# Long-convolution block with feed-forward on one core: new layout of the short convolution, row pairs in the second product, two more tiles transposed by DMA, and a new order

## The chip, the cores and the metric

One core of a Trainium2 chip. The metric is the device time of one execution in microseconds (us). TensorE is called PE (PEld is its loading of weights), VectorE DVE, ScalarE ACT, GpSimd POOL, and SyncE SP; SP here only issues DMAs. PSUM has eight banks of 512 32-bit words per partition.

## The reference

Inputs and output are bfloat16; S = 2048 tokens, D = 640 channels, F = 1728.

```python
def _A_ref(q, k, v, shift_k, ssm_k, ssm_D):
    k_shift = sum of k delayed by t (t = 0..3) * shift_k[:, t]      # causal, 4 taps
    kv = k_shift * v
    y = irfft(rfft(kv, 2S) * rfft(ssm_k, 2S))[:S]                   # long causal convolution per channel
    y = y + kv * ssm_D
    return q * y

def _B_ref(x, w1, b1, w2):
    h = x @ w1 + b1
    return (h * tanh(softplus(h))) @ w2

x = A_q
h = x + _A_ref(layernorm(x), A_k, A_v, A_shift_k, A_ssm_k, A_ssm_D)
out = h + _B_ref(layernorm(h), B_w1, B_b1, B_w2)
```

## The kernel before

**Stages.** The channels are five blocks of 128 (written m or b below), in three chunks: blocks 0 and 1, blocks 2 and 3, block 4. The long convolution is a Fourier transform in two stages of matmuls, a product, and an inverse in two stages:

- `k1pe`, `k1ev`: the filter `A_ssm_k` of one block, transposed on PE (eight transposes per half unit), and copied from PSUM. `dadd` then adds the skip term `ssm_D` to tap 0, one row of 128 values.
- `ktpe`, `ktev`, `ktsh`: the same for `A_k`, in groups of 32 channels; POOL makes a copy shifted by one column for the taps that reach into the tile before.
- `wsh`, `coef`, `cfpe`: band matrices of the short filter's taps, built by POOL from a mask and `coef`. `kspe` multiplies them with the transposed k: for each of 20 channel groups and four steps `a` one matmul of 128 columns and one of 96. `kv` (DVE) multiplies the result in PSUM with v.
- `s1kpe`/`s1vpe`: stage 1 of the transform for filter and signal, pairs of matmuls of 64 weight columns each. `s2kpe`/`s2vpe`: stage 2, with the table G (4 MB, loaded as `d_g0` to `d_g7`).
- `sw`: DMAs that copy the filter's spectrum with partitions swapped in pairs. `p2`, `p1`: products of the signal's spectrum with the swapped and the plain filter, by DVE or POOL.
- `i1pe`: first inverse stage. `i2pa`, `i2pb`, `i2pc` (one per chunk, for each of 16 token tiles): second inverse stage, with the table t2m (1 MB).
- Per token tile of 128 tokens: `ln1` (first norm's statistics), `ln1p`, `lnx`, `y` (PSUM copy), `wb` (times the normed x), `h` (plus x), `bn`, `pow`, `hc` (second norm), and a transpose into `lnhT`.
- Feed-forward in units of 256, 256, 512, 512, 512 tokens: `m1pe` (13 column blocks of w1, five matmuls each), `hb` (ACT: Mish), `m1pex` (the last 64 of the 1728 columns, two groups side by side in PE's columns), `m2pe` (per tile two halves of 320 columns, 14 matmuls each), `res` (plus h), `d_out` (store).

A name ends in x or y for the two halves of a unit. Evacuations of PSUM (names with `ev`, and `y`) are copies by ACT or DVE.

**Transposes of the second norm.** Tiles 0 to 3 (units 0 and 1) are transposed on PE (`trpe`, five transposes at line 850) and copied by ACT or DVE (`trev`). Tiles 4 to 15 go by a transposing DMA on SP's queue (`trd`, line 839).

**The 64-row remainder of the second product.** w2 has 13 blocks of 128 rows and one of 64. The last matmul of each `m2pe` (line 916) uses all 128 rows of `hbx`, whose halves hold different tokens, against w2 padded with zeros in the other half:

```python
_, lhs, h = last64[t2]
nc.tensor.matmul(po[:, 0:d1 - d0], lhs, w2h[:, d0:d1] if h else w2[:, 13, d0:d1], start=False, stop=True)
```

The zeros are written by POOL (`w2z`, `w2hz`).

**Order.** The text `ORDER` names some 1030 steps, each with its engine (t PE, a ACT, v DVE, p POOL, d SP's DMA queue, s ACT's DMA queue). Each engine works through its own steps in that order; a planner (`_schedule`) with estimated durations merges them into one sequence of emission and gives out the PSUM banks. DMAs of SP are issued in the order's sequence, and each waits for its inputs at SP. DVE and POOL products are kept from running at the same time by a small POOL copy (`turn`).

Of the kernel before, what the change touches and what calls it, by code (L numbers as in the profile page):

```python
# [16 lines left out]
S = 2048  # L17
D = 640
# [8 lines left out]
d_id:s d_sk:s wz:v d_dr:s cz:v d_go:d d_n2:d wm:t fz0:t d_n0:d k1pe2x:t warm:a k1ev2x:a d_n3:d k1pe2y:t d_n1:d cfpe:t d_n4:d k1pe0y:t k1ev0y:a  # L27
k1pe0x:t k1ev2y:v dadd2:v s1kpe2_0x:t k1ev0x:v kz:p coef:v s1kpe2_2x:t s1kpe2_1x:t s1kpe2_1y:t s1kev2_1x:v s1kev2_0x:v s1kev2_1y:v s1kpe2_3y:t
s1kev2_3y:a k1pe3x:t k1ev3x:a s1kev2_2x:a k1pe1x:t k1ev1x:v k1pe1y:t w2hz:p dadd0:p wsh0:p dadd1:p k1pe3y:t dadd3:p k1pe4y:t k1ev1y:v k1pe4x:t
k1ev3y:v k1ev4x:v dadd4:p s1kpe1_2y:t k1ev4y:a s1kpe1_3x:t s1kpe1_0x:t s1kev1_0x:v s1kpe1_0y:t s1kpe1_1x:t s1kev1_1x:v s1kpe0_1x:t s1kpe1_3y:t  # L30
s1kpe4_0y:t s1kev1_2y:a s1kpe2_2y:t s1kev1_3x:a d_k3:d d_k2:d d_x0:d s1kev0_1x:a s1kev1_0y:v s1kev1_3y:a s1kev2_2y:a s1kpe3_0x:t s1kpe0_2y:t
s1kev0_2y:a s1kpe0_1y:t s1kev3_0x:a s1kpe2_3x:t s1kev2_3x:a ktpe3y:t s1kpe0_2x:t s1kpe4_2x:t s1kev4_2x:a s1kev4_0y:v ln1_2:v s1kev0_1y:v ln1_1:v
s1kpe4_1x:t s1kpe0_0x:t s1kev4_1x:a s1kpe4_2y:t s1kpe1_2x:t s1kev0_0x:v s1kpe0_0y:t d_k1:d d_g4:d s1kev1_2x:a d_k0:d d_g5:d s1kpe3_2x:t ktpe0y:t
s1kev0_2x:a ktpe1y:t d_v1:d ktev0y:v ktpe4y:t ktev3y:v s1kpe4_0x:t ktev1y:v ktev4y:v s1kev4_2y:a s1kev0_0y:a s1kev3_2x:a s1kpe3_1y:t s1kev4_0x:a
s1kev3_1y:a s1kpe3_3x:t s1kpe3_0y:t s1kpe4_1y:t s1kev3_3x:a s1kpe0_3y:t s1kpe4_3y:t s1kpe2_0y:t s1kpe4_3x:t s1kev0_3y:v s1kev2_0y:v s1kev4_1y:a
ln1_3:v s1kev3_0y:a s1kev4_3x:a wsh1:p s1kpe3_2y:t ln1p1:p s1kpe3_1x:t s1kpe1_1y:t ktsh1:p wsh3:p s1kpe0_3x:t s1kpe3_3y:t s1kev3_1x:a ktpe2y:t
s1kev0_3x:a s1kev4_3y:a s1kev3_2y:v s1kev1_1y:v ktpe4x:t ktpe3x:t ktev3x:v ktpe1x:t s1kev3_3y:a ktev1x:v ln1_0:v ktpe0x:t s2kpe_14y:t d_g6:d d_g0:d
ktev2y:a ktpe2x:t d_g7:d d_g1:d ktev4x:a s2kpe_13x:t s2kev_13x:a s2kpe_15y:t s2kpe_12y:t s2kev_12y:a ktev0x:a s2kev_15y:a kspe4_1x:t ktev2x:v kv4_1x:v
# [104 lines left out]
class _Op:  # L143
    def __init__(self, name, opts, deps, allocs, uses, emit, prio, lat):
# [12 lines left out]
        self.start = None  # L157
        self.eng = None
        self.done = False
        self.tiled = name.startswith("s1") and "pe" in name or name.startswith("m1pex")  # L160
# [14 lines left out]
def _schedule(ops):  # L175
# [7 lines left out]
    for word in ORDER:  # L183
# [6 lines left out]
        for rt in o.allocs:  # L190
            t, rt.slot = rt.ring.free()
            est = max(est, t)
# [34 lines left out]
def _dve1(n):  # L227
    return 0.06 + 0.001045 * n
# [740 lines left out]
```

## Time and profile before

| what | value |
|---|---|
| runs | 224.22, 224.60, 224.79 us; median 224.6 |
| profiled execution | 224.86 us, span 223.1 us |
| granted clock of PE | 1.00 |
| busy: PE, DVE, ACT, POOL | 214.7, 146.2, 134.4, 65.7 us |
| HBM read, written | 20.45 MB, 2.62 MB |
| first transposes of the filter on PE | at 5.71 us |
| first evacuation of a stage-1 product | at 9.50 us |
| last matmul of the first inverse stage | 89.5 us |
| PE's last matmul | 219.8 to 220.0 us |

Busy time is the sum over an engine's instructions; on PE the ends of matmuls are modelled, so a matmul that waits may count as busy. Where many matmuls follow each other, the distance from start to start is the better measure. Where instructions of ACT or DVE follow each other without a gap, the length of the whole run over their number is the step.

### The profile page before, as it was taken

To read this page: it belongs to the slowest core of one execution; us is meant where nothing else is said; L and a number is where in the kernel's file an instruction comes from. 1 tells how busy PE (TensorE), PEld (TensorE's weight loads), DVE (VectorE), ACT (ScalarE), POOL (GpSimd) and SP (SyncE) were. 2 spreads that over 40 slices of the span, in tenths; PEclk is the share of its full clock that TensorE was granted. 3 is DMA by queue.
4 is the path that set the end of the run, shared out by engine and by line. 5 is a ranking of instruction groups with operands and counts; after the bars stand their busy time and mean duration, and the time that the engine had idled before them with its cause. 6 is when DMAs were issued, how large, how long until landed. Compare 5 with 4: busy or idle time off the path is not lost.

```text
span 223.1 us, 6218 instructions
## 1 busy us (share of the span) xinstructions
PE 214.7 (96%) x2598; PEld 162.1 (73%) x2598; DVE 146.2 (66%) x317; ACT 134.4 (60%) x268; POOL 65.7 (29%) x106
## 2 busy tenths in 40 slices
PE   7998899999999999999999999999999999999994
PEld 2988899999877999988887644576645445675773
DVE  0699989999999998999788898974400000004023
ACT  2689989999999999888870446800053454330000
POOL 1271950005596007235767714320000000000000
PEclk9999999999999999999999999999999999999999
DMA  6999991075999999100001401043350000000024
GB/s 214 388 408 424 408 413 69 3 203 193 277 290 283 319 351 347 62 3 0 3 0 32 88 0 31 0 91 60 88 179 0 1 0 3 0 0 0 32 82 153
DMA packets 27342, 30.68 MB, mean 138 GB/s; under 512 B 9393, under 2 KB 23730, under 8 KB 26930
## 3 DMA queue, kind: packets, MB, share of 16 engines
q1 hardware_dynamic: 26880, 30.10, 41.1%
q8 instruction: 20, 0.33, 0.6%
q10 hardware_dynamic: 338, 0.18, 0.3%
q14 instruction: 8, 0.07, 0.1%
q0 software_dynamic: 96, 0.00, 0.0%
HBM read 20.45 MB, written 2.62 MB: 103 GB/s over the span
## 4 chain that ended last, share of the span: by engine, by line
PE 64%; DVE 13%; DMA 7%; ACT 7%; POOL 5%; issue 2%; SPq 0%; DVEq 0%; ACTq 0%; POOLq 0%
PE ps L915 21%; PE ps L898 19%; ACT uv L419 6%; DMA x<-in_A_q_dram 5%; PE ps L743 4%; PE ps L744 4%; PE ps L652 3%; PE ps L543 2%; PE ps L571 2%; DMA rn<-in_A_ssm_k_dram 2%; DVE st L776 2%; DVE st L822 2%; PE ps L595 2%; POOL r L782 2%; PE ps L916 2%
## 5 line engine op out<-in xcount | busy, mean ns | idle before, releaser
L915 PE MATMUL ps<-rn,uv 128*128 128x320 bf16 (+2 forms) x416 | 61.1, 299 | 0.2 <-DVE x L921 0.2
L903 ACT ACTIVATE uv<-ps,b1s 128x512 bf16<-128x512 f32 (+1 forms) x65 | 35.4, 610 | 39.1 <-PE ps L898 38.5
L898 PE MATMUL ps<-G 128*128 128x512 bf16 (+1 forms) x325 | 58.6, 337 | 0.0
L915 PEld LDWEIGHTS <-uv 128*128 128x128 bf16 x416 | 40.2, 98 | 17.5 <-issue 0.4
L419 ACT CAST uk<-ps 128x512 bf16<-128x512 f32 (+1 forms) x96 | 48.7, 702 | 2.6 <-PE ps L544 1.6
L898 PEld LDWEIGHTS <-G 128*128 128x128 bf16 x325 | 31.2, 98 | 23.9 <-issue 1.1
L921 DVE TENSOR_TENSOR xb<-ps,xb 128x320 bf16<-128x320 f32 (+2 forms) x12 | 5.7, 487 | 36.3 <-PE ps L916 35.8
L419 ACT CAST uv<-ps 128x512 bf16<-128x512 f32 (+2 forms) x57 | 28.7, 845 | 0.0
L921 DVE TENSOR_TENSOR xa<-ps,xa 128x320 bf16<-128x320 f32 x12 | 5.9, 488 | 21.6 <-PE ps L916 21.6
L827 POOL TENSOR_TENSOR r<-ve,mhalf 128x1 f32<-128x1 f32 x16 | 10.0, 630 | 32.7 <-DVE ve L824 32.7
L743 PE MATMUL ps<-a,uv 128*128 128x128 bf16 x160 | 18.8, 219 | 0.2
L421 DVE CAST uk<-ps 128x512 bf16<-128x512 f32 (+1 forms) x27 | 17.2, 669 | 1.4 <-PE ps L744 0.9
L743 PEld LDWEIGHTS <-uv 128*128 128x128 bf16 x160 | 17.9, 113 | 0.0
L421 DVE CAST uv<-ps 128x512 bf16<-128x512 f32 (+1 forms) x25 | 15.3, 677 | 0.0
L685 PE MATMUL ps<-uv,G 128*128 128x64 bf16 (+1 forms) x256 | 12.8, 197 | 0.8
L685 PEld LDWEIGHTS <-G 128*128 128x128 bf16 x256 | 11.1, 96 | 3.1 <-issue 2.1
L600 DVE TENSOR_TENSOR ra<-ps,rb 128x512 bf16<-128x512 f32 x20 | 12.5, 684 | 0.3 <-PE ps L596 0.3
L419 ACT CAST rb<-ps 128x512 bf16<-128x512 f32 (+1 forms) x28 | 10.6, 495 | 2.7 <-PE ps L803 2.7
L652 PE MATMUL ps<-uk,G 128*128 128x160 bf16 x128 | 12.1, 230 | 0.0
L782 POOL TENSOR_TENSOR r<-ve,mhalf 128x1 f32<-128x1 f32 x16 | 10.8, 672 | 1.3
L706 DVE TENSOR_TENSOR uv<-uv,uk 128x2048 bf16<-128x2048 bf16 (+1 forms) x11 | 10.9, 1022 | 0.0
L544 PE MATMUL ps<-cst,ra 128*64 128x128 bf16 x160 | 10.6, 220 | 0.1
(116 smaller groups left out, 376.7 us busy)
## 6 DMA issues: line engine op xcount, KB each, us to landing
G<-tab_g SPq DMA_DIRECT2D x8, 512.0 KB, 12.9
rn<-in_A_ssm_k_dram SPq DMA_DIRECT2D x5, 512.0 KB, 6.2
ra<-in_A_k_dram SPq DMA_DIRECT2D x4, 640.0 KB, 9.9
rb<-in_A_v_dram SPq DMA_DIRECT2D x2, 1280.0 KB, 13.1
G<-in_B_w_dram SPq DMA_DIRECT2D x5, 432.0 KB, 6.4
rn<-in_B_w_dram SPq DMA_DIRECT2D x1, 2080.0 KB, 9.8
rn<-uk SPq DMA_DIRECT2D x4, 512.0 KB, 5.1
rb<-uk SPq DMA_DIRECT2D x8, 256.0 KB, 7.9
```

Of the source, the lines that this page charges most:

```text
L419: nc.scalar.copy(o, i)
L421: nc.vector.tensor_copy(o, i)
L600: nc.vector.tensor_tensor(kv_w[:, m, :, 8 * h:8 * h + 8, l0:l0 + n], ps.rearrange("p (l t d) -> p d t l", l=n, t=8), raw_v[:, 8 * h:8 * h ...
L652: nc.tensor.matmul(ps[:, o:o + 160], g_v[:, f, :], KA[:, :, f, :], start=True, stop=True)
L685: nc.tensor.matmul(ps[:, fl * n:fl * n + n], g_v[:, f0 + h * kf + fl, :], VX[x][:, :, f0 + h * kf + fl, :], start=True, stop=True)
L706: eng.tensor_tensor(v, v, K[c.i][:, :, f0:f1, :], ALU.mult)
L743: nc.tensor.matmul(pz[:, k, :], V[c.i][:, dg // 4, :, dg % 4], a12[:, 0, :], start=True, stop=False)
L782: nc.gpsimd.tensor_tensor(r1[:, t2:t2 + 1], ve1[:, t2:t2 + 1], mhalf[:, 0:1], ALU.pow)
L898: nc.tensor.matmul(ph[:, 0:w], w1[:, dc, fc * P:fc * P + P], lnhT_of(u)[:, dc, 0:w], start=(dc == 0), stop=(dc == NDC - 1))
L903: nc.scalar.activation(hb_of(u)[:, fc, 0:w], rt.tile[:, 0:w], ACT.Mish, bias=b1s[:, fc:fc + 1], scale=1.0)
L915: nc.tensor.matmul(po[:, 0:d1 - d0], hb_of(u)[:, fc, tl * P:(tl + 1) * P], w2[:, fc, d0:d1], start=(fc == 0), stop=False)
L921: nc.vector.tensor_tensor(x, rt.tile[:, 0:d1 - d0], x, ALU.add)
```

## The change

- **Second norm, tiles 2 and 3.** Unit 1 also takes the transposing DMA: `trd2`, `trd3` in place of `trpe2`, `trpe3`, `trev2`, `trev3`.
- **Short convolution by 8 steps of 16 channels.** `kt_s` holds eight groups of 16 channels x 8 times each, in two steps and the shifted one; the band matrices are ten (block, half) of 704 elements in place of four of 1120; the second matmul has 48 columns in place of 96. The two groups of a channel quarter go to alternate words of PSUM. `coef` is made whole on PE (`cfpe`: nine small matmuls, where one was) and copied by ACT in one instruction.
- **Skip term as a column.** `ssm_D` is loaded as a column per block (`d_col`: block 0 on ACT's queue, the others on POOL's, `d_dp`), and `dq` adds it on DVE to column 0 of the raw filter, ahead of the first half's transposes.
- **Row pairs.** The 64-row remainder of four output pieces (two tiles, one in each half of `hbx`) is a group of its own, `m2q`, ahead of the 13 other matmuls: 64 rows each, from rows 0 to 63 and 64 to 127 in turn, into four banks. `m2pe` adds its 13 matmuls to these. The memsets of w2 are gone. `m1pex0` and `m1pex2` split each unit's tokens over the two halves, as `m1pex1` did.
- **Swap and products of chunk 0**: four DMA pieces in place of two, eight products of 1024 elements in place of four of 2048, for p1 and p2 each.
- **First filter block**: now block 0, in two halves on SP's and ACT's queues; ACT's half is issued before cst. Block 2 was first, on SP's queue.
- **A new total order**, with other engines for many steps: 48 go from ACT to DVE and 45 from DVE to ACT. In SP's sequence t2m moves from between the swaps to behind w1 and the third x load; `d_x1` moves ahead of w2.

The diff, without `ORDER` and the planner's constants:

```diff
-    wsh = [t.rearrange("p (g n) -> p g n", n=224) for t in [xb[:, i * 1120:(i + 1) * 1120] for i in range(3)] + [hc_t[:, 0:1120]]]
-    kt_s = [uv[i][:, 4096 * m:4096 * m + 2560].rearrange("p (g a t) -> p g a t", g=4, a=5) for i, m in ((0, 0), (0, 1), (1, 0), (1, 1), (1, 2))]
+    at_uv = [uv[i][:, 4096 * m:4096 * m + 4096] for i, m in ((0, 0), (0, 1), (1, 0), (1, 1), (1, 2))]
+    kt_s = [t[:, 0:3072].rearrange("p (g a t) -> p g a t", g=8, a=3) for t in at_uv]
+    wsh = [[x.rearrange("p (e l n) -> p e l n", e=2, l=2) for x in (t[:, 3072:3776], xb[:, 704 * m:704 * m + 704])] for m, t in enumerate(at_uv)]
...
-        for _ in range(9):
+        for _ in range(8):
             nc.tensor.matmul(ps[:, 0:512], wz[:, 0:P], wz[:, P:D], start=True, stop=True)
...
     def emit_act_dmas(e):
+        nc.scalar.dma_start(raw_n[0][64:P], n_view[0, 16:32])
         nc.scalar.dma_start(cst[:], dram["cst"])
-        nc.scalar.dma_start(sk_r[:], A_shift_k.rearrange("(d n) j -> d (n j)", n=20))
-        nc.scalar.dma_start(d_row, A_ssm_D.unsqueeze(0))
+        nc.scalar.dma_start(d_col[:, 0:1], d_view[0])
+        nc.scalar.dma_start(sk_r[:], A_shift_k.rearrange("(d n) j -> d (n j)", n=40))
+    def emit_dp(e):
+        for m in range(1, NDC):
+            nc.gpsimd.dma_start(d_col[:, m:m + 1], d_view[m])
...
-    cf_pe = OP("cfpe", ("pe", 0.1), [d_id, d_sk], allocs=[cf_rt], emit=emit_cfpe, prio=-3)
+        for i, (a, j0, j1) in enumerate(((0, 0, 4), (4, 0, 4), (7, 1, 4), (7, 0, 1), (1, 0, 4), (2, 0, 4), (3, 0, 4), (5, 0, 4), (6, 0, 4))):
+            nc.tensor.matmul(ps.rearrange("p (r t) -> p r t", t=11)[:, :, a + j0:a + j1], cst[0:16, 3 * P - 16 * a:4 * P - 16 * a],
+                             sk_r[:].rearrange("p (r j) -> p r j", j=4)[:, :, j0:j1], start=(i == 0), stop=(i == 8))
...
-                for l in (2 * k, 2 * k + 1):
-                    r = 4 * m + l
-                    for a in (2 * h, 2 * h + 1):
-                        o = ps[:, (l - 2 * k) * 256 + (a - 2 * h) * P:][:, 0:P]
-                        nc.tensor.matmul(o, t[:, l, a, :], wsh[r // 5][:, r % 5, 0:128], start=True, stop=False)
-                        nc.tensor.matmul(o[:, 0:96], t[:, l, a - 1 if a else 4, :], wsh[r // 5][:, r % 5, 128:224], start=False, stop=True)
+                for l in range(2):
+                    for e in range(2):
+                        o, q, w = ps[:, 256 * l + e:256 * l + 256:2], 4 * e + 2 * k + l, wsh[m][k][:, e, l, :]
+                        nc.tensor.matmul(o, t[:, q, h, :], w[:, 0:128], start=True, stop=False)
+                        nc.tensor.matmul(o[:, 0:48], t[:, q, 0 if h else 2, :], w[:, 128:176], start=False, stop=True)
...
-            (nc.vector if e == "dve" else nc.gpsimd).tensor_tensor(k, k, rd, ALU.add)
+            nc.vector.tensor_tensor(n[:, 0:1], n[:, 0:1], d_col[:, b:b + 1], ALU.add)
...
+        n = (4, 2, 2)[ci]
...
-        npf = (32, 32, 32)[len(c.dcs) - 1]
+        npf = (16, 32, 32)[c.i]
...
-        if U_OF[t2] >= 2:
+        if U_OF[t2] >= 1:
             def trd(t2=t2, hc_rt=hc_rt):
...
+            def pq(e, ab=ab, parts=parts):
+                for i in range(2):
+                    for t2 in ab:
+                        _, c, h = last64[t2]
+                        d0, d1, rt = parts[t2][i]
+                        rhs = w2h[64:P, d0:d1] if h else w2[0:64, 13, d0:d1]
+                        nc.tensor.matmul(ps_f32(rt)[:, 0:d1 - d0], hbx[64 * h:64 * h + 64, c:c + P], rhs, start=True, stop=False)
...
-                        nc.tensor.matmul(po[:, 0:d1 - d0], hb_of(u)[:, fc, tl * P:(tl + 1) * P], w2[:, fc, d0:d1], start=(fc == 0), stop=False)
-                    nc.tensor.matmul(po[:, 0:d1 - d0], lhs, w2h[:, d0:d1] if h else w2[:, 13, d0:d1], start=False, stop=True)
+                        nc.tensor.matmul(po[:, 0:d1 - d0], hb_of(u)[:, fc, tl * P:(tl + 1) * P], w2[:, fc, d0:d1], start=False, stop=(fc == NFC - 2))
```

SP's sequence around the end of the front, before:

```text
... sw1_0 sw1_1 d_t2m sw2_0 sw2_1 d_w11 d_w14 d_w12 d_w13 d_w10 d_w2 d_x1 trd4 ...
```

and after:

```text
... sw0_1 d_g6 sw0_0 sw2_0 sw0_2 sw0_3 sw1_1 sw1_0 sw2_1 d_w14 d_w12 d_x2 d_w11 d_w13 d_w10 d_t2m d_x1 d_w2 trd2 trd3 trd4 ...
```

More of the change, by code (lines that the diff above doesn't have):

```diff
@@ L215, in _schedule @@
                 o.behind = last
-        for rt in o.allocs:
-            rt.ring.take(rt.slot, rt)
         order.append(o)
@@ L494 @@
[L494 to L501 removed]
+        ps = ps_f32(cf_rt)[:, 0:440]
```

304 lines of the change are left out of this document (157 added, 147 removed).

## The prediction

> **What bounds the kernel now.** I read the page first, then the table of stretches, then the order of time of each engine, the DMA issues last. The page's busy shares:
>
> ```profile
> PE 214.7 (96%) x2598; PEld 162.1 (73%) x2598; DVE 146.2 (66%) x317; ACT 134.4 (60%) x268; POOL 65.7 (29%) x106
> ```
>
> 96% of PE proves little, since a matmul that waits for a bank can count as busy; the stretches (busy us, instructions in brackets, in the order PE, PEld, DVE, ACT, POOL, then granted clock, DMA share, GB/s) say more:
>
> ```profile
> 10.00:15.00 5.00, 4.50 (x106) 4.35 (x106) 5.00 (x9) 3.98 (x7) 3.62 (x5) 1.00 1.01 399
> 30.00:35.00 5.00, 5.00 (x93) 5.00 (x91) 4.98 (x9) 5.00 (x11) 1.49 (x3) 1.00 0.84 333
> 60.00:65.00 5.00, 4.56 (x102) 4.21 (x100) 5.00 (x9) 5.00 (x12) 4.82 (x3) 1.00 1.03 287
> 80.00:85.00 5.00, 5.00 (x93) 5.00 (x91) 4.51 (x8) 5.00 (x11) 0.09 (x1) 1.00 1.01 347
> 170.00:180.00 10.00, 10.00 (x48) 4.57 (x47) 0.00 (x0) 6.05 (x11) 0.00 (x0) 1.00 0.00 1
> ```
>
> Up to 90 us ACT and DVE are both full: the front is bound by emptying PSUM. From 15 to 80 us they lose about 1.3 us (ACT) and 1.9 us (DVE) in all. Late in the span both are idle for long and PE alone works. How tight PE is there is read from its order of time (start, length, matmuls of one line merged):
>
> ```profile
> 89.54 6.77 PE L803 MATMUL ps<-uk,ra 128*128 128x256 bf16 x66
> 96.15 0.44 PE L850 MATMUL ps<-cst,hc 128*128 128x128 bf16 x5
> 96.43 0.60 PE L803 MATMUL ps<-uk,ra 128*128 128x256 bf16 x4
> ...
> 114.13 1.93 PE L915 MATMUL ps<-rn,uv 128*128 128x320 bf16 x13
> 115.89 0.30 PE L916 MATMUL ps<-rn,hbx 128*128 128x320 bf16 x1
> ...
> 131.39 0.74 PE L878 MATMUL ps<-G 128*64 128x256 bf16 x10
> 132.06 3.41 PE L898 MATMUL ps<-G 128*128 128x512 bf16 x15
> ```
>
> Start to start, 13 matmuls of 320 columns take 1.76 us (0.136 each), 15 of 512 take 3.24 (0.216), five transposes 0.28. From the last matmul of the inverse transform (89.5) to PE's last (220.0) are 130.5 us. The work listed there is the t2m products 8.8, transposes 1.1, first product of the feed-forward 14.2 + 42.1, its 64-row remainder (L878) 2.5, second product 32 x 1.907 = 61.0: 129.7. So PE has under 1 us of slack in 130, and two sums decide: when PE gets out of the front, and how much PE work is behind it.
>
> **The change, part by part.**
>
> *Start.* The first filter block's load ends at 5.66 us (0.72 + 4.94 in the chain), and ACT's first evacuation of a stage-1 product starts at 9.50. Now block 0 comes in two halves from SP's and ACT's queues; one issue costs SP 0.7 us (five in 3.50), so a half saves some 0.35. Behind it on ACT's queue stand cst, the skip column and the short filter; the transposes need cst, the first half's also dq0. Both copies of the block go to DVE (0.64 each; before, ACT took 1.01 for one), and the row add is gone (DVE 0.21, hop 0.3). I take -0.8 for the whole start; ends -1.4 (load and copies both in full) and +0.5 (cst or the column lands later than the block did). The Trainium skill, "DMA: Bandwidth & Descriptors", Rules for kernel authors, says two transfers to disjoint partition halves run on the same engines and serialize; by that the load gains nothing, the start would be -0.4 and the sum 0.4 less.
>
> *PSUM evacuation and products of the front.* I add up each engine's list to the last evacuation of the inverse transform, at the steps the rows show:
>
> ```profile
> 53.41 16.56 ACT L419 CAST uv<-ps 128x512 bf16<-128x512 f32 x34
> 59.33 4.23 DVE L421 CAST uv<-ps 128x512 bf16<-128x512 f32 x7
> 70.75 2.35 DVE L706 TENSOR_TENSOR uv<-uv,uk 128x2048 bf16<-128x2048 bf16 x2
> ```
>
> That is 0.487 (ACT) and 0.604 (DVE) per 512 columns, 1.18 for a product of 2048, 0.62 for 1024 (0.60 to 0.69 apart in that list). Before: ACT 81.6, DVE 80.1. After: 79.8 and 79.3. DVE's products of chunk 0 go from 6 x 1.18 to 9 x 0.62 (-1.5); coef goes from 1.0 on DVE to 0.43 on ACT; one kt copy goes from ACT to DVE (-0.4); the rest is small. 2.5 us less on two engines: -1.25, if the idle time stays. Ends: -3.2 (the idle from 9.5 on, some 2.0 us per engine, goes too) and +1.0 (the new order adds 2 us of idle).
>
> *POOL* gets more: band matrices 10 x 1.30 (704 elements at 2065 ns per 1120) for 4 x 2.07; shifts 5 x 1.2 for 5 x 0.61; 7 products at 2.05 for 2 at 4.07; four column DMAs at 0.5 to 0.77; four row adds (0.45) and two memsets (0.62) go. Its list to the end of the front goes from 27 to 38 us of 87, and it waited 21.4 us there for one evacuation: hidden, cost 0. Behind a wsh or ktsh that is late wait kspe on PE; the first needs eight wsh, two shifts and one ln1p, 14.2 us after coef at about 9, so 23.5 against 29.4, where the first kspe stands now. If that cover is gone, what is late counts in full.
>
> *Short convolution on PE.* 80 second matmuls shrink from 96 to 48 columns (0.045 each now): at most -1.8, in a stretch where PE has about 6 us of slack in 41, so 0. Their outputs now lie on every second word of PSUM, which no row shows: 0 to +3.4 (all 128 columns at double the 0.055, less the shrink). Eight more small matmuls for coef, one warm-up fewer and four more fillers are under 1 us of the same slack.
>
> *t2m moved.* Before, SP issued it at 64.6, ahead of w1; now behind w1 and x2, which wait for the last second-stage matmul. I put that at 70: the list's running sum there is 64, and the clock is some 7 ahead of the sum (8 before, less the start). 2.2 + 0.98 + 1.05 MB at 349 GB/s (mean of 75 to 90 us) is 12.1, and about 3 until a load has landed (xa's 960 KB take 6.1, of which 2.8 is flow): 85.5. i2pa0 needs it when 35 half units of inverse transform are done, 35 x 0.446 = 15.6, so at 86. I charge 0.3; ends 0 and +2.1 (295 GB/s, the mean of 54 to 90).
>
> *Tiles 2 and 3 by DMA.* Two groups of transposes leave PE: -0.56, and two copies of 0.5 to 0.7 leave ACT. Two issues join SP's queue, behind w2. A transposing DMA lands 2.6 us after its issue:
>
> ```profile
> ra<-tab_t2m SPq DMA_DIRECT2D x1, 1024.0 KB, 8.6
> xa<-in_A_q_dram SPq DMA_DIRECT2D x1, 960.0 KB, 6.1
> G<-hc SPq DMA_TRANSPOSE x12, 2.6
> ```
>
> DVE's list from the first wb to hc3 is 10.5 us (before 12.5, with three other items between), so hc3 ends 11.7 after the front and tile 3 lands near 14.6; PE reaches m1pex0 after 8.2 + 0.56 + 7.1 = 15.9. Cost 0; each us that hc3 is later than 1.3 costs one.
>
> *Row pairs.* 32 matmuls at 0.137 (4.4 us) become 8 groups of four 64-row matmuls. Row pairs are not in the trace; column pairs are: L878's ten take 0.67 where five steps of 0.109 are 0.55, so pairs run together and one excursion costs 0.12. Like that, a group is 2 x 0.136 + 0.12 = 0.39: -1.2. Ends: -2.2 (no excursion cost) and +1.0 (no overlap). m1pex0 and m1pex2 take the same pairs: 0. Four banks per group are held early; the second product empties a bank in 0.49 against 1.9 per bank on PE: 0.
>
> *End.* The last piece is now 320 columns (0.49) and a whole tile's store, not 128 columns (0.29): +0.2.
>
> Sum: -0.8 - 1.25 + 0.3 - 0.56 - 1.2 + 0.2 = -3.3. The profiled execution took 224.86 (span 223.1, 1.8 around it), so 221.6; it is 0.26 over the median 224.6, which gives 221.3.
>
> **Rivals.**
> 1. *The new order idles the front.* Where evacuations wait in a row, the start's and the lists' 2.05 are lost: 221.3 + 2.05 = 223.3. For: 93 steps change between ACT and DVE, and every engine works in order. Against: the present order loses under 2 us per engine from 15 to 80.
> 2. *The slots open.* The front takes its far end, the row pairs theirs: 221.3 - 2.0 - 1.0 = 218.3. For: the swap comes in quarters, the products in eighths.
> 3. *Row pairs run one after the other*: +2.2, 223.5. For: no row shows them. Against: column pairs overlap.
> 4. *The strided PSUM writes double the matmul*: +3.4, no slack taking it: 224.7, no change. The Trainium skill, "PSUM — Partial Sum Buffer", Specifications, gives PSUM lines of 8 bytes, with any non-contiguous pattern slowing matmuls significantly. By that rule this case happens; no run here shows it yet.
> 5. *Slower: t2m comes late.* PE stands before i2pa0, the chain of the tokens behind it. It decides from 3.6 us of wait, t2m landing after 89.6. If the swap's transfers are still running when w1 is issued, 1.6 MB of them at 290 GB/s put 5.5 in front: it lands at 91, a wait of 5: 221.3 - 0.3 + 5 = 226.0. Against: the last first-stage filter copy stands at 47 of the list's sum, so near 54, and 3.1 MB of swap at 285 GB/s end near 66.
>
> **How the numbers follow.** Forecast 0.45, rivals 1 to 5: 0.15, 0.11, 0.07, 0.07, 0.15. The time is the likeliest: 221.3. A difference under 0.3% (0.7 us) can't be told from none. Faster: forecast, 2, 3 and most of 1, 0.75; the same: 4 and the edge of 1, 0.09; slower: 5 and a little of 4, 0.16. With the bounds above, the forecast's own range is 219.5 to 223; with rivals 1, 3 and 4 whole and half of 2 it is 218.3 to 225.2, leaving out most of 5 and half of 2.
>
> **What would show it.** Right: the first stage-1 evacuation near 8.7; the last inverse-transform matmul near 87.3; no gap on PE before the first t2m product; L850 with 10 matmuls; a row-pair group at 0.39 start to start; from there to PE's last about 128.7. Wrong: PE waiting for the DMA of t2m or of the transposes, kspe steps above 0.055, or idle on both evacuating engines between 15 and 70.

## The result, and the profile after

The kernel after takes **235.72 us** (median of four executions, 235.23 to 236.45), the kernel before 224.66 on the same chip (224.22 to 224.79): ratio 1.0499, 95% interval 1.0467 to 1.0531. Forecast were 221.3, with a range of 218.3 to 225.2; the slowest rival stood at 226.0. The profiled execution took 236.45, span 234.6. Ratios leave out executions over 1.5% above the fastest of their kernel (three of j's ten); medians and ranges keep them.

| place | before | forecast | after |
|---|---|---|---|
| first evacuation of a stage-1 product, us | 9.50 | 8.7 | 15.08 |
| last matmul of the first inverse stage | 89.5 | 87.3 | 101.3 |
| from its end to the end of PE's last matmul | 130.3 | 128.7 | 130.0 |

So the loss of 11 lies before 101 us, and the gain expected behind that is missing too. The same stretches as before the change (PE, PEld, DVE, ACT, POOL busy; granted clock, DMA share, GB/s):

```profile
10.00:15.00 5.00, 4.08 (x37) 3.40 (x39) 1.45 (x3) 0.00 (x0) 0.00 (x0) 0.50 1.02 423
30.00:35.00 5.00, 4.92 (x104) 4.37 (x104) 4.26 (x10) 4.26 (x9) 4.54 (x7) 1.00 0.27 65
60.00:65.00 5.00, 5.00 (x87) 4.75 (x85) 4.10 (x8) 4.44 (x11) 4.92 (x3) 1.00 0.56 134
80.00:85.00 5.00, 4.60 (x73) 3.87 (x71) 4.73 (x7) 5.00 (x13) 0.45 (x1) 1.00 1.01 296
```

From 10 to 15 ACT does nothing and PE runs 37 instructions at a granted clock of 0.50, where it ran 106 at 1.00. The chain that ended last, in its first 16 us, tells why (start, length, what):

```profile
0.73 0.65 ACTq L475
1.42 0.60 ACTq L476
2.05 8.52 DMA d_col<-in_A_ssm_D_dram
10.71 0.17 DVE rn L627
10.93 1.07 PE ps L633 x8
12.00 1.47 PE ps L499 x9
13.47 1.00 PE ps L633 x8
```

The kernel waits 8.5 us for 128 elements of the skip column. The DMA issues up to 3 us (queue, count, KB each, median us to landing) show what it stood with:

```profile
rn<-in_A_ssm_k_dram ACTq DMA_DIRECT2D x1, 256.0 KB, 3.8
cst<-tab_cst ACTq DMA_DIRECT2D x1, 128.0 KB, 4.4
...
d_col<-in_A_ssm_D_dram ACTq DMA_DIRECT2D x1, 0.2 KB, 8.5
sk_r<-in_A_shift_k_dram ACTq DMA_DIRECT2D x1, 5.0 KB, 8.3
```

Before, cst landed in 2.1 and the short filter in 3.8. Later, in the short convolution, PE's order of time has a second new cost, and DVE's a third:

```profile
39.11 0.27 PE L606 MATMUL ps<-xb,uv 128*128 128x128 bf16 x1
39.18 0.25 PE L607 MATMUL ps<-xb,uv 128*128 128x48 bf16 x1
39.25 0.29 PE L606 MATMUL ps<-xb,uv 128*128 128x128 bf16 x1
39.33 0.25 PE L607 MATMUL ps<-xb,uv 128*128 128x48 bf16 x1
```

```profile
10.71 0.16 DVE L627 TENSOR_TENSOR rn<-rn,d_col 128x1 bf16<-128x1 bf16 x1 [9.51 <-DMA d_col<-in_A_ssm_D_dram]
...
16.54 2.35 DVE L627 TENSOR_TENSOR rn<-rn,d_col 128x1 bf16<-128x1 bf16 x3
```

```profile
16.18 5.35 POOL L513 TENSOR_TENSOR xb<-cst,coef 128x704 bf16<-128x704 bf16 x4 [12.33 <-ACT coef L420]
```

A pair of 128 and 48 columns takes some 0.15 from start to start (0.149 on average over the pairs that the trace holds). Before, 128 and 96 columns took 0.10:

```profile
41.50 0.22 PE L595 MATMUL ps<-xb,uv 128*128 128x128 bf16 x1
41.56 0.21 PE L596 MATMUL ps<-xb,uv 128*128 128x96 bf16 x1
41.60 0.22 PE L595 MATMUL ps<-hc,uv 128*128 128x128 bf16 x1
```

The first addition to the filter's column 0 takes 0.16 alone; three that run while POOL builds its band matrices take 2.35. Of these the middle one takes 0.15, the others 1.02 and 1.34, and they end at 17.56 and 18.89, as POOL's first two products do (17.54 and 18.87).

### The profile page after: what moved, and what is told of

Same layout as the page of the kernel before. It is cut to its first block, busy times and chain, and to the rows that moved or that the text cites. A ratio compares the mean times of both kernels' runs of the same rounds, so it can differ in the third digit from the quotient of the medians.

```text
span 234.6 us, 6285 instructions
## 1 busy us (share of the span) xinstructions
PE 222.6 (95%) x2608; PEld 166.8 (71%) x2619; DVE 148.0 (63%) x323; ACT 133.7 (57%) x263; POOL 76.2 (32%) x115
## 4 chain that ended last, share of the span: by engine, by line
PE 76%; ACT 6%; DMA 6%; POOL 5%; DVE 4%; issue 2%; SPq 1%; ACTq 1%; DVEq 0%
PE ps L908 21%; PE ps L941 19%; PE ps L558 6%; PE ps L660 4%; PE ps L606 4%; DMA d_col<-in_A_ssm_D_dram 4%; PE ps L753 4%; PE ps L811 4%; PE ps L754 3%; ACT uk L420 3%; ACT uv L420 2%; PE ps L695 2%; PE ps L633 2%; DMA rb<-uk 2%; PE ps L559 2%; POOL r L790 2%
## 5 line engine op out<-in xcount | busy, mean ns | idle before, releaser
L941 PE MATMUL ps<-rn,uv 128*128 128x320 bf16 (+2 forms) x415 | 58.4, 299 | 0.1
L420 ACT CAST uk<-ps 128x512 bf16<-128x512 f32 (+2 forms) x94 | 48.4, 639 | 16.5 <-PE ps L559 12.6
L913 ACT ACTIVATE uv<-ps,b1s 128x512 bf16<-128x512 f32 (+1 forms) x65 | 34.3, 603 | 32.4 <-PE ps L908 32.2
L941 PEld LDWEIGHTS <-uv 128*128 128x128 bf16 x416 | 39.2, 98 | 18.5 <-issue 1.6
L422 DVE CAST uk<-ps 128x512 bf16<-128x512 f32 (+1 forms) x29 | 18.8, 669 | 4.4 <-PE ps L559 3.2
L835 POOL TENSOR_TENSOR r<-ve,mhalf 128x1 f32<-128x1 f32 x16 | 9.9, 621 | 25.1 <-DVE ve L832 25.1
L753 PEld LDWEIGHTS <-uv 128*128 128x128 bf16 x160 | 17.9, 113 | 0.0
L720 POOL TENSOR_TENSOR rn<-rn,uv 128x1024 bf16<-128x1024 bf16 x5 | 10.6, 2122 | 15.6 <-ACT uv L420 15.6
L633 PE MATMUL ps<-cst,rn 128*128 128x128 bf16 x80 | 6.8, 246 | 5.5 <-DVE rn L627 4.4
L716 DVE TENSOR_TENSOR uv<-uv,uk 128x1024 bf16<-128x1024 bf16 (+1 forms) x14 | 11.1, 837 | 0.0
L633 PEld LDWEIGHTS <-rn 128*128 128x128 bf16 x80 | 6.1, 151 | 6.9 <-DVE rn L627 4.5
## 6 DMA issues: line engine op xcount, KB each, us to landing
rn<-in_B_w_dram SPq DMA_DIRECT2D x1, 2080.0 KB, 12.5
```

The costliest lines, as they stand in the source:

```text
L420: nc.scalar.copy(o, i)
L422: nc.vector.tensor_copy(o, i)
L633: nc.tensor.transpose(ps[:, t2, :], n[:, 8 * h + t2:S:16], ident)
L716: eng.tensor_tensor(v, v, K[c.i][:, :, f0:f1, :], ALU.mult)
L753: nc.tensor.matmul(pz[:, k, :], V[c.i][:, dg // 4, :, dg % 4], a12[:, 0, :], start=True, stop=False)
L913: nc.scalar.activation(hb_of(u)[:, fc, 0:w], rt.tile[:, 0:w], ACT.Mish, bias=b1s[:, fc:fc + 1], scale=1.0)
```

## The experiments

All ratios are to the kernel before on the same chip. In c to f L626, L605, L606 and L512 are the lines L627, L606, L607 and L513 of the kernel after; in the later kernels lines move by a few, and the operands tell which they are.

### The start and the PSUM words: a, b, c, d

Theories: the late column (start), the alternate PSUM words, the new order. b, and with it d, e, f and j, pairs channels otherwise than the reference does, so these five do not compute it; a leaves out block 0's skip term.

a_no_column:
```diff
-        nc.scalar.dma_start(d_col[:, 0:1], d_view[0])
+        nc.gpsimd.memset(d_col[:, 0:1], 0.0)
```


> Block 0's skip column is set to zero by POOL instead of loaded (the skip term of block 0 is left out), the changed kernel otherwise. Theory 1a, the 2-byte column itself is what is late and the loads behind it on ACT's queue come late only because of it: the short filter lands near 5 us, the first stage-1 evacuation moves from 15.1 to about 8.5, and the time falls by 5 to 6 us, to about 230. Theory 1b, everything that stands on ACT's queue behind the half block and cst lands late beside the bulk loads: the short filter still lands near 10.5, the small matmuls of coef then hold PE until there, the first stage-1 evacuation comes near 13, and the time falls by 1 to 2.5 us, to about 234.

b_words_in_row:
```diff
-  o = ps[:, 256 * l + e:256 * l + 256:2]
+  o = ps[:, 256 * l + 128 * e:256 * l + 128 * e + 128]
```


> The short convolution's two channel groups go to 128 consecutive words of PSUM each, not to alternate words (the products then pair the wrong channels with v; instruction counts and shapes stay). Theory 2, the alternate words cost the matmuls their step (0.074 us each in the changed kernel's trace, 0.0525 in the one before): the step falls to about 0.048, 160 of them give back 3.5 to 4 us of PE time, and as PE has no slack there the time falls by 3 to 4 us, to about 232. Rival: the step falls but PE waits for evacuations instead, and the time falls by under 1 us.

c_whole_block:
```diff
-        nc.scalar.dma_start(raw_n[0][64:P], n_view[0, 16:32])
-        return lambda: nc.sync.dma_start(raw_n[b], n_view[b]) if b else nc.sync.dma_start(raw_n[0][0:64], n_view[0, 0:16])
+        return lambda: nc.sync.dma_start(raw_n[b], n_view[b])
```


> Block 0 of the filter comes whole from SP's queue again; ACT's queue issues cst, the column, the short filter in this order. Theory 1b: the column is issued at 1.3 instead of 2.05 us with only cst ahead of it, lands near 6, the first stage-1 evacuation comes near 9 and the time falls by 5 us, to about 230.5. Theory 1c, small descriptors land late beside bulk loads wherever they stand in the queue: the column lands near 9.5 to 10, and the time falls by at most 1.5 us, to about 234.5.

d_whole_and_row has the edits of b and c.

> Both edits: the whole block from SP's queue and consecutive words in PSUM. If the start and the PSUM writes are separate losses, their gains add: about 226.5 to 227 if theory 1b and theory 2 hold. Theory 3, the new order has a loss of its own (the v load and three G pieces wait at SP for block 2's stage 1 until 32.7 us, and the last swap pieces arrive late): the sum stays over the kernel before by 2 to 3 us.

| run | median us (range) | ratio (interval) | first stage-1 evacuation |
|---|---|---|---|
| a | 232.51 (231.12 to 232.65) | 1.0326 (1.0284 to 1.0369) | 10.92 |
| b | 231.57 (230.70 to 232.49) | 1.0299 (1.0256 to 1.0341) | 14.96 |
| c | 231.48 (231.11 to 232.08) | 1.0289 (1.0249 to 1.0329) | 10.66 |
| d | 226.56 (226.25 to 227.94) | 1.0096 (1.0057 to 1.0136) | 8.74 |

The contiguous words alone bring 4.2 us, the whole block alone 4.2, both 9.2: theories 1b and 2, and not 1c. Theory 3 is not settled by d, which is still 1.6 over the kernel before. The last column holds a second effect: a and c began with PE at half speed, d did not (their nine matmuls of the coefficients took 1.54, 1.54 and 0.88; see the last section), so the 1.9 us between c's first evacuation and d's is not the work of the PSUM words.

a lies between its two forecasts. The short filter, issued at 2.05 in the column's place, landed at 7.17, after 5.1 us, where the column had taken 8.5; so the place in the queue is not all of the column's delay. What else made it late is not separated. In c, the issues up to 3 us:

```profile
cst<-tab_cst ACTq DMA_DIRECT2D x1, 128.0 KB, 2.1
...
d_col<-in_A_ssm_D_dram ACTq DMA_DIRECT2D x1, 0.2 KB, 4.7
sk_r<-in_A_shift_k_dram ACTq DMA_DIRECT2D x1, 5.0 KB, 5.4
```

With the half block off ACT's queue and the column one issue earlier, it lands at 5.8 and not at 10.6. In d's order of time the words in a row take some 0.08 a pair (0.084 on average):

```profile
34.60 0.22 PE L605 MATMUL ps<-xb,uv 128*128 128x128 bf16 x1
34.66 0.18 PE L606 MATMUL ps<-xb,uv 128*128 128x48 bf16 x1
34.68 0.22 PE L605 MATMUL ps<-xb,uv 128*128 128x128 bf16 x1
```

By the averages the gain is (0.149 - 0.084) x 80 pairs = 5.2 of PE's time, of which 4.2 showed.

### What is left in d: e, f, j

e_no_skip leaves out the skip term; f_g_first issues three pieces of G ahead of v; j_no_columns is e without the loads of the column.

```diff
-            nc.vector.tensor_tensor(n[:, 0:1], n[:, 0:1], d_col[:, b:b + 1], ALU.add)     # e
+            pass
-            nc.gpsimd.dma_start(d_col[:, m:m + 1], d_view[m])                              # j, and ACT's load
+            pass
- ... d_v0:d ... d_g5:d d_g0:d ... d_g7:d ...                                               # f
+ ... d_g5:d d_g0:d d_g7:d d_v0:d ...
```

> This is the kernel with whole first block and contiguous words (d_whole_and_row, 226.56), without the five 128x1 additions of the skip column: the skip term is left out of the result. It asks what these additions hold up. Theory A: they are where the front's missing time went. In d the three that run together took 2.68 us of VectorE, with 1.32 us of waiting for loads ahead of them, and the fifth one about 0.8; all evacuations queued behind them wait. Taken out, some 4.8 us of VectorE are free, half of that if ScalarE and VectorE share the front evenly: 2.4 us, so 224.2, and the last inverse-transform matmul goes from 92.4 to about 90. Theory B: the front is late because of what SP's queue holds behind block 0 of v and because of the order; then the additions only fill waits that are there anyway: 226.0 to 226.6. Theory C: the clock granted to TensorE early on is the bound: no change either.

> d_whole_and_row (226.56) with the loads of G's pieces 5, 0 and 7 issued ahead of v's first half instead of behind it; nothing else moves. In d SP waited with v's first half until 28.3 us, for block 2's stage 1, and G's pieces stood behind that; the DMA engines fell to 227 GB/s in 25 to 30 us. Theory B (SP's queue is where the front's time went): G's pieces land about 5 us sooner, the stage-2 matmuls that need them no longer wait: 1.5 to 3 us less, 223.5 to 225. Theory A (the additions on VectorE) and theory C (the clock): within 0.5 of 226.6, since the pieces were there in time for the matmuls that their place in the order allowed.

> e_no_skip (225.27, no skip term in the result) without the five loads of the skip column, 128 elements of 2 bytes each. In e the second to fourth load of the long kernel took 7.2, 7.9 and 8.1 us to land, in the kernel before 5.8, 6.5 and 7.1, and the DMA engines moved 237 GB/s in the first 10 us against 290. Theory D (the small loads hold up the large ones beside them): the four loads land about 1 us sooner, both evacuating engines idle less between 9 and 20, and the time falls by 0.7 to 1.3: 224.0 to 224.6. Rival (the new order of the front idles by itself): within 0.3 of 225.3.

| run | median us (range) | ratio (interval) |
|---|---|---|
| e | 225.27 (224.79 to 227.80) | 1.0033 (1.0012 to 1.0054) |
| f | 226.28 (225.70 to 227.59) | 1.0067 (1.0044 to 1.0090) |
| j | 224.64 (224.14 to 227.81) | 1.0001 (0.9977 to 1.0026) |

The additions cost 1.3 to 1.4 us: theory A, at half its size. That is read from the times; e's profiled execution (227.80) is the slowest of its eleven and began at half speed, so its trace does not show the gain. G's early pieces bring at most 0.3, and the intervals of f and d overlap. In both profiles the last matmul of the first inverse stage stands at 92.4, but f's began at half speed and 1.9 us later (first evacuation 10.67 against 8.74), so they cannot be compared. On theory C see the last section. The waits that A names, in d:

```profile
11.21 2.68 DVE L626 TENSOR_TENSOR rn<-rn,d_col 128x1 bf16<-128x1 bf16 x3 [1.32 <-DMA rn<-in_A_ssm_k_dram]
```

```profile
9.84 5.35 POOL L512 TENSOR_TENSOR xb<-cst,coef 128x704 bf16<-128x704 bf16 x4 [6.00 <-ACT coef L420]
```

From e to j the time falls by 0.6, which the intervals do not separate; the trace does show the small loads beside the large ones. First 10 us, first d, then j:

```profile
0.00:10.00 10.00, 8.54 (x103) 5.71 (x105) 2.57 (x6) 2.64 (x5) 3.10 (x15) 1.00 0.68 240
```

```profile
0.00:10.00 10.00, 8.29 (x105) 5.36 (x105) 2.31 (x5) 2.82 (x5) 0.86 (x11) 1.00 0.81 285
```

With five loads of 128 two-byte elements the DMA engines move 240 GB/s, without them 285; the fourth load of the filter lands in 8.3 (d) and 7.0 (j). It is so in every profile: 225 to 244 GB/s in the eleven kernels with such loads (a has four of them), 279 to 293 in the nine without.

### Transposing DMA alone, the right pairing, and two repairs: h, i, k, l, m

h_before_tr is the kernel before with `if U_OF[t2] >= 1`, so with tiles 2 and 3 by DMA and nothing else.

> The kernel before, with one part of the change alone: token tiles 2 and 3 of the second norm by transposing DMA in place of five transposes on TensorE and an evacuation each; the rest of the order stays. By the prediction's term: 0.56 us less on TensorE, the evacuations off ScalarE, so about 224.1. The rival: a transposing DMA of tile 3 lands 2.6 us or more after the normalised tile, where transposing on TensorE and the evacuation took about 1; the step of 64 features that covers tiles 0 to 3 stands near the end of unit 0's first layer, and waits: up to 2 us more, 226.5. In d, TensorE's step of the 64 features began at 108.74, about when tile 3's DMA landed.

i_right_row is d with the channels paired as in the reference: a half step takes one parity.
```diff
-  o, q = ps[:, 256 * l + 128 * e:256 * l + 128 * e + 128], 4 * e + 2 * k + l
+  o, q = ps[:, 128 * l:128 * l + 128], 4 * k + l
-  kv_w[:, m, :, 8 * h:8 * h + 8, l0:l0 + n]
+  kv_w[:, m, k:32:2, 8 * h:8 * h + 8, :]
```


> d_whole_and_row with the channels paired as the reference has them: one half of a short-convolution step now takes the channels of one parity, so that its 4 groups of 128 words stand contiguously in PSUM, and VectorE's product writes every second group of channels. Instructions, their counts and their order are those of d. All theories: as d, 226.1 to 227.0, if VectorE's product of 512 words costs the same with its output striding over two groups (0.06 us at most on each of 20 steps otherwise, 1.2 us on VectorE in all, 0.6 on the time).

k_pe_tr is i with `if U_OF[t2] >= 2` and the two tiles' transposes back in the order.

> i_right_row (227.18) with token tiles 2 and 3 of the second norm transposed on TensorE and evacuated by ScalarE as in the kernel before; the two steps stand where the tiles are ready in this order. If the transposing DMA is what the back lost: h_before_tr lost 1.1 by this part alone, where 0.56 less was forecast, and in i the step of 64 features began at 107.83, when tile 3 had landed. So 1.1 less, 226.1, and from the last inverse-transform matmul to TensorE's last matmul 129.3 or less in place of about 130.3. If in this order something else held that step too (ScalarE's queue of Mish evacuations): 227 or more, since five transposes and an evacuation of 0.75 come back on the two engines for each tile.

l_pool_skip is i with the additions on POOL, ahead of the band matrices; m_combo is i with the edits of k, l and f.

> i_right_row (227.18) with the five additions of the skip column on GpSimd, ahead of its first band matrices, so that VectorE's evacuations don't wait behind them. e_no_skip showed 1.3 us for taking them out. Theory A (VectorE's wait beside GpSimd's band matrices): most of that comes back, 226.0 to 226.4, with some 0.5 us each on GpSimd, whose band matrices then start 1 to 2 us later but are needed at 33 us only. Rival: GpSimd's additions wait for the loads of the long kernel and the transposes of blocks 1 to 3 wait for GpSimd instead: 227 to 228.

> i_right_row with the changes of k_pe_tr and l_pool_skip, and G's pieces 5, 0 and 7 ahead of v's first half as in f_g_first: a kernel that computes all of the reference. If the three savings add up (1.1, 0.8 to 1.2, 0.3): 224.6 to 225.0, about the kernel before. If the front's idle time is set by the order and the loads of the column, less comes back: 225.5 to 226.5.

| run | median us (range) | ratio (interval) |
|---|---|---|
| h | 225.82 (225.44 to 225.91) | 1.0041 (1.0024 to 1.0059) |
| i | 227.18 (225.77 to 228.32) | 1.0103 (1.0069 to 1.0138) |
| k | 225.82 (225.57 to 227.94) | 1.0090 (1.0050 to 1.0129) |
| l | 225.71 (225.35 to 227.71) | 1.0060 (1.0037 to 1.0082) |
| m | 225.66 (225.48 to 226.03) | 1.0045 (1.0018 to 1.0073) |

In the old order this part alone loses 1.1 us. The order of time of PE in h shows where:

```profile
105.05 0.30 PE L878 MATMUL ps<-G 128*64 128x256 bf16 x1
106.19 0.73 PE L878 MATMUL ps<-G 128*64 128x256 bf16 x9 [0.84 <-DMA G<-hc]
```

The step of 64 features stands with its first matmul done until tile 3 has landed. PE then waits 0.61 more before unit 2, at 128.6, where the kernel before has no such wait. The right pairing costs nothing that shows: i is d, within the intervals. Each repair of k, l and m is of the expected sign, but none is separated from i by its interval, and they do not add up: m was expected at 224.6 to 225.0, and its interval holds l's ratio and overlaps k's. Least shown is k: its ratio is 0.1% under i's, and from the front's end to PE's last it takes 129.9 against i's 130.1, where 129.3 or less was expected.

### The skip term as a row, fillers: n, o, p, q

n_row_skip is m with the skip term as in the kernel before (one load of 1.2 KB, added by POOL to the evacuated block):
```diff
+            nc.gpsimd.tensor_tensor(kd, kd, rd, ALU.add)      # kd: tap 0 of the transposed block, rd: its 128 of the row
```
o_row_fill moves two filler matmuls (`fz0`) to behind `wm`; p_row_dma is o with tiles 2 and 3 by DMA; q_row_later is o with the fifth addition behind three more band matrices.

> All of the reference. From the kernel after the change: first block whole on SP's queue, contiguous words with the right pairing, G's pieces ahead of v's first half, tiles 2 and 3 transposed on TensorE, and the skip term as a row again: one load of 1.2 KB, added by GpSimd to the transposed block as in the kernel before. j_no_columns (no skip term at all, transposing DMA) was at 224.6. Theory D (small loads and the additions ahead of the transposes are what the front lost) with the transposes on TensorE worth 1.1: about 223.5, under the kernel before (224.65). If GpSimd's additions behind the evacuations hold stage 1 instead, or if the transposes on TensorE give nothing in this order: 224.6 to 225.6.

> n_row_skip with two of the filler matmuls moved from the middle of stage 2 to the place behind the first filler, where the kernel before has them; TensorE then works until 5.4 instead of 4.84 us, and the first block lands between 5.2 and 5.8. In the profiles whose first block landed at 5.7 TensorE had stood idle for 0.97 us and the 9 matmuls of the coefficients then took 1.54 instead of 0.88, the first evacuation of stage 1 came at 10.8 instead of 8.9. Theory E (the gap costs TensorE its speed, and with it about 2 us in some executions): the higher times of the kernel's executions, 2 us above its median in l and j, are gone, and the median is the same or up to 0.5 lower. Rival: the gap is only a sign of late loads, and nothing changes.

> o_row_fill with tiles 2 and 3 of the second norm by transposing DMA again, so that this part of the change is measured on a base that has the row pairs and the new order. By the prediction's term it is 0.56 faster than o_row_fill; by h_before_tr (the step of 64 features waits for tile 3's DMA) it is 0.5 to 1.3 slower.

> o_row_fill (228.74) with GpSimd's fifth addition of the skip row behind three more of its band matrices. In o GpSimd stood with that addition for 5.29 us, until block 4 was evacuated at 20.3, the band matrices behind it were late, and TensorE waited for them 2.0 and 1.8 us at the short convolution. If that is the whole of o's loss: 3 to 3.8 less, 225.0 to 225.7. If the additions hold stage 1 itself: 227 or more.

| run | median us (range) | ratio (interval) |
|---|---|---|
| n | 229.53 (228.47 to 230.41) | 1.0208 (1.0177 to 1.0239) |
| o | 228.74 (228.53 to 230.34) | 1.0190 (1.0161 to 1.0218) |
| p | 229.05 (228.77 to 230.26) | 1.0202 (1.0174 to 1.0229) |
| q | 225.50 (225.39 to 226.00) | 1.0048 (1.0030 to 1.0066) |

n missed its forecasts by 4 to 6 us; o and p, forecast from n and o, share that loss. The reason is one of their own, which o's order of time of POOL shows, and q removes with its 3.2 us:

```profile
20.30 0.46 POOL L628 TENSOR_TENSOR rn<-rn 1x128 bf16<-1x128 bf16 x1 [5.29 <-DVE rn L423]
```

POOL stood 5.29 us with that addition, the band matrices behind it came late, and PE waited 1.99 and 1.76 at the short convolution. o against n and p against o are inside their intervals, and o still has an execution at 230.34: theory E is not shown.

### What the rest of the change is worth: r, s

r_bare_pe and s_bare_dma hold no skip term and no loads for it; otherwise they are i with f's edit and o's fillers, r with the transposes of tiles 2 and 3 on PE, s with the change's DMA.

> No skip term in the result, no loads for it; first block whole, right contiguous words, G's pieces first, fillers ahead of the first block, tiles 2 and 3 transposed on TensorE: what the rest of the change is worth without the parts found to cost. j_no_columns was at 224.64, with a part of its executions at 227.7; the transposes on TensorE are worth 1.1 by h_before_tr, the pieces of G 0.3. So 223.2, 0.6% under the kernel before: then the change's savings (row pairs 1.2, fewer evacuations 1.25) are real and were outweighed. If the new order itself idles the front: 224.2 to 225.

> r_bare_pe with tiles 2 and 3 by transposing DMA as in the change. By the prediction's term 0.56 faster than r_bare_pe, by h_before_tr 1.1 slower, by o against p (229.05 against 228.74) 0.3 slower.

r: 224.65 (224.15 to 225.18), ratio 1.0008 (0.9993 to 1.0023). s: 224.44 (223.90 to 224.92), ratio 0.9992 (0.9977 to 1.0007). Both are the kernel before, and each other, within the intervals: on this base the DMA neither gains nor loses. r was expected at 223.2, or at 224.2 to 225 if the new order itself idles the front; it is the second. So the savings of the rest are smaller than forecast, and the traces of r, s and the kernel before say which. In r, PE around a group of row pairs:

```profile
206.48 0.71 PE L937 MATMUL ps<-rn,uv 128*128 128x320 bf16 x4
207.12 0.31 PE L925 MATMUL ps<-rn,hbx 64*128 64x320 bf16 x1
207.12 0.31 PE L925 MATMUL ps<-w2h,hbx 64*128 64x320 bf16 x1
207.26 0.30 PE L925 MATMUL ps<-rn,hbx 64*128 64x320 bf16 x1
207.26 0.30 PE L925 MATMUL ps<-w2h,hbx 64*128 64x320 bf16 x1
207.49 0.58 PE L937 MATMUL ps<-rn,uv 128*128 128x320 bf16 x3
```

and the weight loads of the same 0.8 us:

```profile
207.11 0.11 PEld L925 LDWEIGHTS <-hbx 64*128 64x128 bf16 x4 [0.27 <-issue]
207.49 0.39 PEld L937 LDWEIGHTS <-uv 128*128 128x128 bf16 x4 [0.27 <-issue]
```

Four matmuls from 206.48 at 0.136 end their turn at 207.02, so the group holds PE from 207.02 to 207.49: 0.47, with 0.10 lost ahead of it and 0.10 behind, since neither switch has its weights loaded ahead. All eight groups of r show the same 0.10 and 0.38.

The fronts, s and then the kernel before, in two stretches each:

```profile
0.00:20.00 20.00, 18.62 (x304) 14.77 (x305) 11.33 (x25) 12.84 (x21) 10.81 (x18) 1.00 0.93 350
20.00:88.88 68.88, 67.21 (x1391) 62.51 (x1390) 66.83 (x111) 67.08 (x139) 34.35 (x36) 1.00 0.73 235
```

```profile
0.00:20.00 20.00, 17.40 (x314) 13.78 (x315) 12.27 (x29) 12.99 (x22) 6.87 (x17) 1.00 0.93 351
20.00:89.70 69.70, 67.23 (x1373) 63.42 (x1371) 67.08 (x106) 68.27 (x142) 29.36 (x31) 1.00 0.81 269
```

DVE and ACT together work 158.1 us in s and 160.6 before: 2.5 less, as forecast. But they idle 15.8 of their first 40 us in s and 14.7 before; from 20 us to the end of the front 3.9 and 4.1.

## Why the prediction was wrong, by its own steps

- **Start, -0.8, end +0.5: the step that failed most.** The worst end named was that "cst or the column lands later than the block did". It did, but by 5 us: the column landed at 10.6, the first stage-1 evacuation came 5.6 later than before. The sum of queue and small load was never bounded; the forecast priced the half's issue and not what stands behind it. Undoing it (c) is worth 4.2. A part of the 5.6 is PE's speed after its wait for the column: from the start of the nine matmuls to the marker are 3.15 us (11.93 to 15.08) at a granted clock of 0.50, in d 1.91 (6.83 to 8.74) at 1.00. No term stood for that. The two halves gained the load nothing: the later one landed at 5.6 us, a whole block at 5.0 (d) and 5.6 (c). The rule cited there from the Trainium skill, "DMA: Bandwidth & Descriptors", Rules for kernel authors (halves of the partitions serialize), agrees with that. But the loss was not there.
- **Start, the marker.** Even in s, whose first stage-1 evacuation comes at 8.30, the start gains nothing: by 20 us its two evacuating engines have idled 1.1 us more than before, not 1.6 less. Before, ACT and DVE had copied two whole transposed blocks ahead of that marker, in s only one; the earlier marker has less work behind it. The term was +0.55 in place of -0.8.
- **Strided PSUM, taken as 0: it was rival 4.** The pair of matmuls takes 0.15 in place of 0.08, and b shows 4.2 us on the clock. "Slack of 6 us in 41" did not take it: from the first short-convolution matmul to the last that the traces hold, PE idles 0.05 of 25.4 us, ACT 3.8 and DVE 3.3, in b 0.5, 0.5 and 0.4 of 21.0; PE had become the limit there. The rule of the Trainium skill, "PSUM — Partial Sum Buffer", Specifications (TRN2), that non-contiguous patterns slow matmuls significantly, agrees with this trace. A chance of 0.07 for it was too low, with a rule for it and no row against it.
- **Lists of ACT and DVE, -1.25: right in size, eaten by a term not in it.** Without the skip additions the lists are 2.5 us shorter. With them DVE's list is 3.6 longer (81.6 in d, 78.0 in e): they were counted at next to nothing (0.16 is what one alone takes), and POOL, "hidden, cost 0", held them. e prices this at 1.3 to 1.4 us.
- **Tiles 2 and 3, -0.56, "each us that hc3 is later than 1.3 costs one".** For that step the reckoning held: in the new order hc3 ended 12.5 us after the front (s: 101.4 against 88.9; forecast 11.7), 0.8 late, and PE came to the step with no wait. In the old order (h) it ended 14.1 after the front, tile 3 landed behind PE's arrival, and the wait took the place of the transposes: +1.1. What failed is that the 0.56 would come off the time: r and s cannot be told apart, because PE waited 0.52 more before unit 2, whose tiles also come by DMA. r has no wait there. From s:

```profile
127.47 1.24 PE L904 MATMUL ps<-G 128*128 128x512 bf16 x5 [0.52 <-DMA G<-hc]
```

- **Row pairs, -1.2: right mechanism, wrong size.** The group itself is 0.38 start to start, as forecast (0.39), so the pairs do run together. The excursion was taken once, 0.12, from column pairs; it is 0.10 on either side. Each group saves 4 x 0.136 - 0.47 = 0.07, eight of them 0.6. r's back agrees: 129.9 from the front's end to PE's last, before 130.3.
- **t2m, +0.3, and rival 5:** PE did not wait for it; 0. It landed at 95.8 for a first use at 101.4 (s: 84.5 and 88.7). The ten transposes on PE were there, and no gap before the first product with t2m.
- **End, +0.2:** its reason was misread, since the last piece is 128 columns in both kernels (0.29 on DVE). From PE's last matmul to the end of the span are 3.0 us before, 3.1 after and 3.3 in s, so the size is right by luck.
- **Rival 1 (the new order idles the front)** is in what stays: the small loads (0.6 by j, not separated) and 1.1 us of idle in the first 20. Behind 20 us the new order loses nothing against the old (3.9 and 4.1).

The sum: after 235.7; start undone and words in a row (d) 226.6; additions out (e) 225.3; their loads out (j) 224.6; the bare rest (s) 224.4. That is 3.1 over the forecast 221.3. The traces hold 2.3 of it: s's profiled execution took 223.90, and from the profiled 224.86 the forecast was 221.6. Start 1.35, row pairs 0.6 and tiles 0.56, less the 0.3 charged for t2m, are 2.2. The other 0.8 is the place of the two profiled executions among their kernels' own: s's is the fastest of twelve, 0.5 under its median, and the one before is 0.3 over its. No version beat the kernel before: with the whole reference the best are l, m and q, 225.5 to 225.7; s, without the skip term, ties.

What stays open: whether the fillers of o matter by themselves. In j three of ten executions took 227.7, in r and s, which have the fillers, none of 24 was above 225.2; but r and s differ from j in other edits too, and o against n shows nothing. Open too is what made the column slower than the short filter in its place.

## What to carry to other kernels

Follow the first microseconds queue by queue: a load of 256 bytes that an early matmul needs can cost more than the bulk loads ahead of it (8.5 us here, against 3.8 and 4.4 for the two ahead of it). Cost a small instruction by what runs beside it and by what queues behind it, not by its own length, and a change of PE's tiling on entry and on exit. Before two traces are compared, see whether their first matmuls ran at the same speed. And when an order is rewritten, compare idle time up to a fixed moment, not the time of a first event.

## What the runs showed of the hardware

- **Small loads behind a half block.** The same 256-byte load on ACT's queue took 8.5 us behind 256 KB and 128 KB, and 4.7 behind 128 KB alone (c). 5 KB in its place behind 256 KB and 128 KB took 5.1 (a).
- **Alternate words of PSUM.** From start to start, a matmul of 128 columns and one of 48 into every second word take 0.08 and 0.07; into words in a row 0.055 and 0.026.
- **DVE beside POOL.** The 128x1 addition with both inputs in SBUF: 0.16 alone; beside POOL's products of 704, which take 1.34 each, one of three took 0.15 and two 1.02 and 1.34; on POOL itself (l) 0.19 each. The Trainium skill, "SBUF — State Buffer", Who interferes with whom, says that a DVE instruction with two SBUF inputs and a reading POOL instruction exclude each other; the trace agrees.
- **PE's speed after a first gap.** The nine matmuls of the coefficients took 0.88 in k and 1.54 in l; ahead of the first transposes PE had stood idle 0.32 and 0.97 us, and in k 0.54 more ahead of the nine:

```profile
5.16 1.29 PE L630 MATMUL ps<-cst,rn 128*128 128x128 bf16 x16 [0.32 <-DMA rn<-in_A_ssm_k_dram]
6.99 0.88 PE L498 MATMUL ps<-sk_r,cst 16*128 16x160 bf16 x9 [0.54 <-DMA sk_r<-in_A_shift_k_dram]
```

```profile
5.80 1.93 PE L630 MATMUL ps<-cst,rn 128*128 128x128 bf16 x16 [0.97 <-DMA rn<-in_A_ssm_k_dram]
7.66 1.54 PE L498 MATMUL ps<-sk_r,cst 16*128 16x160 bf16 x9
```

  The first stage-1 evacuation came at 8.90 and 10.82: a load 0.6 us later became 1.9. All 20 profiles fall into the same two kinds. In the seven (after, a, b, c, e, f, l) where PE stood idle 0.78 to 1.13 us ahead of its first transposes (after and b again for 4.4 and 4.2 ahead of the second), the first stage-1 pairs then started 0.107 apart; in the thirteen where it stood idle at most 0.52 us there, 0.056. No run set that gap by itself, and later gaps of 1.4 to 1.5 us (n, o, p, q, at 15 us) left the step at 0.056, so the length of a gap alone is not the rule. In l's stretch from 7 to 9.2 the granted clock still reads 1.00, and so it does in a, c and f, while after, b and e read 0.50 at their first stage-1 pairs; the distance between equal matmuls is the surer sign.
